# Two tiles padded: where the stationary operands of an attention and MLP kernel lie in SBUF

## The chip, the cores and the metric

The kernel runs on one core of one Trainium2 chip. The metric is device time in microseconds, the median of several runs of one program. One execution was also recorded by the profiler; that execution has a time of its own.

## The reference

Attention with a band mask, then an MLP whose activation is piecewise: zero below -1, a square between, the identity above 1.

```python
def _attn_ref(q, k, v):                      # 8 batches, 8 heads, 576 positions, 64 wide
    scores = scale * np.matmul(q, k.transpose(0, 1, 3, 2))
    ...
    mask_plain = (rel >= 0) & (rel < window)                                  # 32
    mask_dil = (rel >= 0) & (rel < window * dilation) & (rel % dilation == 0) # every 4th
    masks = np.stack([mask_plain if h < H // 2 else mask_dil for h in range(H)], axis=0)
    ...
    return np.matmul(attn, v).astype(np.float32)

def _moe_ref(x, w_in, w_out):                # x 4608 x 512, w_in 512 x 2048, w_out 2048 x 512
    h = x @ w_in
    g = np.where(pos, h, np.where(neg, 0.0, (h + beta) ** 2 / (4.0 * beta)))
    return (g @ w_out).astype(np.float32)
```

## The kernel before

The MLP's 4608 tokens are cut into 9 blocks of 512, its 2048 hidden units into 16 slices of 128. A step is one block t and one slice f, 144 steps in all; layer 2 of a step is issued two steps after its layer 1. Each matrix is split into a high part, rounded to float32r, and a low part, the remainder, and three products stand for one: high by high, and each high by the other's low.

`layer1(t, f)` makes 12 matmuls (four pieces of the 512 input columns, three products each) into one PSUM bank. Its stationary operand is 128 columns of `wi[f]`, its moving operand 512 columns of `xh` or `xl`. The bank is then read by VectorE and ScalarE, which form the activation with the help of the tile `y` and leave it as `gh` (high) and `gl` (low). `layer2(t, f)` makes another 12 matmuls: for each of the four groups m of 128 tokens three products, added over all f into the bank of m. Here the stationary operand is 128 columns of `gh` or `gl`, the moving one the 512 columns of `wo[f]`.

The attention of the first 16 heads runs before and beside the first MLP steps, that of the other 48 beside the later ones. TensorE's and the transfers' order is written out by hand: a table of slots puts scores (L207, L230), transposes (L330) and value matmuls (L365) between the layers of certain steps. VectorE, ScalarE and GpSimd are ordered by a scheduler.

A matmul reads both operands from SBUF: the weights are loaded by an instruction of their own (LDWEIGHTS, in the profile the row PEld), which can run while the matmul before is under way.

Where a tile lies is set by the pools: one region for each tag, in the order in which tags are first asked for, each as long as the first tile of that tag (or its largest); `bufs` regions where a tag has several. The first tag after the constants starts at byte 3136 of a partition, which is 64 modulo 256. What follows, with lengths in bytes, so that the remainder modulo 256 can be followed:

- `pt0`, `pt1` 2304 each (9 x 256), three `xh` and three `xl` of 8192 (32 x 256), `qr` 2304: remainder stays 64
- `kr` 608 x 4 = 2432 (9 x 256 + 128): behind it the remainder is 192
- all `wi` and `wo` but the last 4096 (16 x 256), `vt` 3072, between them two score tiles `c` of 3200 (12 x 256 + 128 each, 256 together), `qs` 2304, `kk` 4864, `m` 2048: remainder stays 192 (64 for the second `c` alone)
- `y`, two `gh`, two `gl` of 2048 each, then the last weight block, `wo15`: 192

Steps within a tile (a piece of 128 columns, a high or low half) are multiples of 512 bytes, so they don't change a remainder in the MLP.

Of the kernel before, what the change touches and what calls it, by code (L numbers as in the profile page):

```python
# [19 lines left out]
F32 = mybir.dt.float32  # L23
# [10 lines left out]
KPAD = S + 32  # L34
CLS = S // DIL
TOK = 512
# [8 lines left out]
def body(ctx, tc, q, k, q2, k2, v, mask, eye, w_in, w_out, out):  # L45
# [4 lines left out]
    pool = ctx.enter_context(tc.tile_pool(name="pool", bufs=1))  # L50
# [15 lines left out]
    def borrow(name):  # L66
        return pool.tile([128, 2 * DM], F32, tag=spare.pop(0), name=name)

    def load_pair(n):

        if 0 < n < H:
            qr, kr = borrow(f"qr{n}")[:, :S], borrow(f"kr{n}")[:, :KPAD]
        else:
            tags = ("qs", "kk") if n % 4 else ("qr", "kr")
            qr = pool.tile([128, S], F32, tag=tags[0], name=f"qr{n}")
            kr = pool.tile([128, KPAD], F32, tag=tags[1], name=f"kr{n}")
        nc.sync.dma_start(out=qr, in_=q[n // 2])
        nc.sync.dma_start(out=kr, in_=k[n // 2])
        for j in range(2):
            r = slice(64 * j, 64 * j + 64)  # L80
            heads[n + j] = dict(qs=qr[r], ks=kr[r])

    def load(n):
        qr = pool.tile([128, S], F32, tag="qr", name=f"qr{n}")
        kr = pool.tile([128, KPAD], F32, tag="kr", name=f"kr{n}")
        nc.sync.dma_start(out=qr, in_=q2[n - native])
        nc.sync.dma_start(out=kr, in_=k2[n - native])
        heads[n] = dict(qr=qr, kr=kr)
# [249 lines left out]
    def xtile(t):  # L338
        if t not in xt:
            xt[t] = (  # L340
                pool.tile([128, NC, TOK], F32R, tag="xh", name=f"xh{t}", bufs=3),
                pool.tile([128, NC, TOK], F32R, tag="xl", name=f"xl{t}", bufs=3),
            )
        return xt[t]
# [51 lines left out]
    def layer1(t, f, cs=range(NC), bank=("h", 2)):  # L396
        xh, xl = xtile(t)
        if cs[0] == 0 and (t, f) not in hps:
            hps[t, f] = ps.tile([128, TOK], F32, tag=bank[0], name=f"h{t}_{f}", bufs=bank[1])
        hp = hps[t, f]  # L400
        terms = [(w, x, c) for c in cs for w, x in ((0, xh), (1, xh), (0, xl))]
        for i, (w, x, c) in enumerate(terms):
            PE.matmul(  # L403
                out=hp,
                lhsT=wi[f][:, w, 128 * c : 128 * c + 128],
                rhs=x[:, c],
                start=c == 0 and i == 0,
                stop=c == NC - 1 and i == len(terms) - 1,
            )
        if cs[-1] < NC - 1:  # L410
            return
        del hps[t, f]
        y = pool.tile([128, TOK], F32, tag="y", name=f"y{t}_{f}")
        gh = pool.tile([128, TOK], F32R, tag="gh", name=f"gh{t}_{f}", bufs=2)
        gl = pool.tile([128, TOK], F32R, tag="gl", name=f"gl{t}_{f}", bufs=2)
        with tc.high_priority(offset=60):
            nc.vector.tensor_scalar(  # L417
                out=y, in0=hp, scalar1=-1.0, scalar2=1.0, op0=ALU.max, op1=ALU.min
            )
            nc.scalar.activation(out=y, in_=y, func=AF.Square, bias=half_t, scale=0.5)  # L420

            activated = nc.vector.tensor_tensor(out=hp, in0=hp, in1=y, op=ALU.max)  # L422
            copied = nc.scalar.copy(out=gh, in_=hp)  # L423
            if t == 0:
                last["g", f] = copied, activated
            nc.vector.tensor_tensor(out=gl, in0=hp, in1=gh.bitcast(F32), op=ALU.subtract)  # L426
        gs[t, f] = gh, gl
# [33 lines left out]
    def after_pair(n):  # L461
        softmax(n)
        softmax(n + 1)
        if n + 4 < native:
            load_pair(n + 4)
        elif n + 4 == native:
            load(native)
        else:
            split(native)
            load(native + 1)  # L470

    def after(m):
        if m < nhead - 1:
            split(m + 1)
        if m < nhead - 2:
            load(m + 2)
        softmax(m)
# [23 lines left out]
    nc.vector.memset(half_t, 0.5)  # L501
    borrow_pts()
    load_pair(0)
    nc.sync.dma_start(out=msk, in_=mask.rearrange("k p j -> p k j"))
    load_pair(2)
    nc.sync.dma_start(out=ident, in_=eye)
    load_pair(4)
# [49 lines left out]
    with tc.manual_schedule(engines={mybir.EngineType.PE, mybir.EngineType.SP}):  # L557
# [25 lines left out]
        early_values(4)  # L583
        second = marks()
        layer1(0, 0, range(2))
        early_values(6)
        third = marks()
        behind(second, ("wi", 2))
        layer1(0, 1, range(2))
        scores_pair(H, 0, 4)  # L590
        scores_pair(H, 4, NQ)
# [9 lines left out]
        for s in range(len(steps) + lag):  # L601
            if s == 3:
                for f, src, name in ((12, w_out, "wo"), (13, w_out, "wo"), (14, w_in, "wi")):
                    fetch(f, src, name)
                for f, src, name in ((14, w_out, "wo"), (15, w_in, "wi"), (15, w_out, "wo")):
                    fetch(f, src, name)
            if 0 < s < NF:
                todo = [("wo", s)]
                if s + 3 < NF:
                    todo.append(("wi", s + 3))  # L610
                behind(last["g", max(s - 2, 0)], *todo)
            if s == 2:
                acc[0] = ps.tile([128, DM], F32, tag="acc0", name="acc0_0")
                spin(14, acc[0])
            if s < 2:
                layer1(*steps[s], range(2, NC))
            elif s < len(steps):
                layer1(*steps[s])
            run(2 * s)
            while l2 <= s - lag and l2 < len(steps):  # L620
                layer2(*steps[l2])
                l2 += 1
            run(2 * s + 1)
# [64 lines left out]
```

## Time and profile before

| what | value |
|---|---|
| median of 3 runs | 938.39 us (937.88 to 938.51) |
| profiled execution, its time | 935.99 us |
| profiled execution, its span | 934.2 us |
| mean granted TensorE clock | 0.997 |
| moved from and to HBM | 73.87 MB in packets, 78 GB/s over the span |

The span runs from the first to the last instruction. A busy time is the time in which an engine had at least one instruction under way; matmuls overlap each other, so their mean duration (some 390 ns for 512 columns) is longer than the distance from one start to the next. That distance is what counts for the time, and it is read from the chain of work or from the starts in the timeline. In the chain, a row gives when a piece began, how long it was, its engine and line, and how many instructions it holds.

The costliest other groups, each with its count, busy time, mean of one, and the idle time before it:

```profile
L255 ACT ACTIVATE c<-c 96x128 f32<-96x128 f32 x330 | 129.0, 392 | 118.3 <-DVE c L181 118.3
L422 DVE TENSOR_TENSOR h<-h,y 128x512 f32<-128x512 f32 x144 | 100.6, 699 | 49.7 <-ACT y L420 48.3
L417 DVE TENSOR_SCALAR y<-h 128x512 f32<-128x512 f32 x144 | 99.3, 689 | 62.7 <-PE h L403 61.3
L426 DVE TENSOR_TENSOR gl<-h,gh 128x512 fp32r<-128x512 f32 x144 | 98.5, 684 | 36.9 <-ACT gh L423 36.9
```

These are the readers of the layer-1 bank and the exponentials of attention; the matmul groups are shown further below.

### The profile page before, as it was taken

How to read it: one execution, taken by the hardware profiler on the slowest of the kernel's cores; microseconds unless marked ns; L12 is line 12 of the kernel's file. 1: busy time of each engine (PE TensorE's matmuls, PEld its weight loads, DVE VectorE, ACT ScalarE, POOL GpSimd, SP SyncE). 2: the span in 40 equal slices, each digit the busy share in tenths (PEclk: the TensorE clock that was granted, in tenths of full speed). 3: DMA queues.
4: the chain of work that ended last, by engine and by line, in shares of the span. 5: the costliest groups of instructions: out<-in, count | busy, mean ns of one | idle time of the engine just before them, and what ended most of it. 6: DMA issues, size and time to landing. Idle time of an engine off the chain costs nothing.

```text
span 934.2 us, 14426 instructions
## 1 busy us (share of the span) xinstructions
PE 914.5 (98%) x4886; PEld 742.9 (80%) x4886; DVE 685.2 (73%) x1982; ACT 487.1 (52%) x1336; POOL 239.8 (26%) x155
## 2 busy tenths in 40 slices
PE   7889989999999999999999999999999999999998
PEld 6777778888888888888888888888888888888886
DVE  6898887888888888788887888888887643334333
ACT  6778856555555555555555565555556322222222
POOL 4566543222222222222222222222222000000000
PEclk9999999999999999999999999999999999999999
DMA  9981002212232223112322223222321010001001
GB/s 345 406 304 45 1 27 83 92 59 64 70 115 70 69 70 95 59 57 70 115 70 70 70 61 101 67 69 70 114 70 44 1 45 1 1 1 46 0 1 46
DMA packets 31018, 73.87 MB, mean 79 GB/s; under 512 B 3520, under 2 KB 3808, under 8 KB 30944
## 3 DMA queue, kind: packets, MB, share of 16 engines
q1 hardware_dynamic: 30944, 72.94, 24.0%
q8 instruction: 39, 0.64, 0.3%
q14 instruction: 35, 0.29, 0.1%
HBM read 63.49 MB, written 9.44 MB: 78 GB/s over the span
## 4 chain that ended last, share of the span: by engine, by line
PE 89%; DVE 6%; ACT 3%; issue 1%; POOL 1%; DMA 0%; DVEq 0%; POOLq 0%; ACTq 0%
PE acc L439 41%; PE h L403 40%; PE s L230 4%; PE o L365 3%; DVE c L181 1%; ACT c L255 1%; DVE wo_raw L123 1%; DVE wo_m L126 1%; DVE wi_m L126 1%; DVE c L298 1%; PE t L330 0%; POOL c L291 0%; PE s L164 0%; DVE xl L350 0%; DVE y L417 0%
## 5 line engine op out<-in xcount | busy, mean ns | idle before, releaser
L439 PE MATMUL acc<-wo,gh 128*128 128x512 f32 x1152 | 384.3, 395 | 0.0
L403 PE MATMUL h<-xh,wi 128*128 128x512 f32 x1152 | 361.0, 394 | 0.8 <-DVE gl L426 0.8
L439 PEld LDWEIGHTS acc<-wo,gh 128*128 128x128 f32 x1152 | 216.2, 188 | 48.3
L403 PEld LDWEIGHTS h<-xh,wi 128*128 128x128 f32 x1152 | 209.4, 188 | 42.6 <-DVE gl L426 1.0
L403 PE MATMUL h<-xl,wi 128*128 128x512 f32 x576 | 227.1, 394 | 0.0
L439 PE MATMUL acc<-wo,gl 128*128 128x512 f32 x576 | 224.9, 391 | 0.0
L143 POOL TENSOR_TENSOR kk<-kr,kk 128x608 fp32r<-128x608 f32 x48 | 94.8, 1974 | 417.7 <-ACT kk L139 417.7
L255 ACT ACTIVATE c<-c 96x128 f32<-96x128 f32 x330 | 129.0, 392 | 118.3 <-DVE c L181 118.3
L420 ACT ACTIVATE y<-y,consts 128x512 f32<-128x512 f32 x144 | 104.1, 723 | 124.7 <-DVE y L417 124.7
L423 ACT CAST gh<-h 128x512 fp32r<-128x512 f32 x144 | 84.4, 586 | 128.2 <-PE acc L439 126.1
L417 DVE TENSOR_SCALAR y<-h 128x512 f32<-128x512 f32 x144 | 99.3, 689 | 62.7 <-PE h L403 61.3
L422 DVE TENSOR_TENSOR h<-h,y 128x512 f32<-128x512 f32 x144 | 100.6, 699 | 49.7 <-ACT y L420 48.3
L403 PEld LDWEIGHTS h<-xl,wi 128*128 128x128 f32 x576 | 108.1, 188 | 25.2
L426 DVE TENSOR_TENSOR gl<-h,gh 128x512 fp32r<-128x512 f32 x144 | 98.5, 684 | 36.9 <-ACT gh L423 36.9
L439 PEld LDWEIGHTS acc<-wo,gl 128*128 128x128 f32 x576 | 108.2, 188 | 21.1
L306 DVE STREAM_TRANSPOSE pt<-c 32x192 f32<-32x192 f32 x288 | 106.0, 368 | 5.7
L249 DVE TENSOR_TENSOR c<-s,msk 96x256 f32<-96x256 f32 (+1 forms) x168 | 61.5, 377 | 39.7 <-PE s L230 38.7
L291 POOL TENSOR_TENSOR c<-c 96x768 f32<-96x768 f32 x56 | 83.1, 1484 | 16.7 <-DVE c L290 16.5
L181 DVE CUSTOM_DVE_ANT_0 c<-s,c 96x128 f32<-96x128 f32 x288 | 70.5, 280 | 1.0
L255 ACT ACTIVATION_READ_ACCUMULATOR c<-c 96x1 f32 x330 | 62.0, 188 | 0.0
L349 ACT CAST xh<-o 128x288 fp32r<-128x288 f32 (+8 forms) x112 | 38.5, 382 | 41.0 <-PE o L365 25.8
L230 PEld LDWEIGHTS s<-kk,qs 128*96 128x96 f32 x288 | 46.4, 161 | 15.7
(57 smaller groups left out, 646.1 us busy)
## 6 DMA issues: line engine op xcount, KB each, us to landing
kr<-k_in SPq DMA_DIRECT2D x56, 304.0 KB, 3.2
qr<-q_in SPq DMA_DIRECT2D x56, 288.0 KB, 2.8
vt<-v_in SPq DMA_DIRECT2D x32, 384.0 KB, 3.9
out<-out SPq DMA_DIRECT2D x36, 256.0 KB, 3.1
wi_raw<-w_in SPq DMA_DIRECT2D x16, 512.0 KB, 9.5
wo_raw<-w_in SPq DMA_DIRECT2D x16, 512.0 KB, 9.9
msk<-mask_in SPq DMA_DIRECT2D x1, 144.0 KB, 3.7
ident<-eye_in SPq DMA_DIRECT2D x1, 36.0 KB, 4.7
```

The lines of the kernel that those rows point to most:

```text
L143: nc.gpsimd.tensor_tensor(out=kk[:, 1], in0=hd["kr"], in1=kk[:, 0].bitcast(F32), op=ALU.subtract)
L230: PE.matmul(out=sv[:, t - t0], lhsT=hd["qs"][:, t * QT : (t + 1) * QT], rhs=hd["ks"][:, :, t * QT : t * QT + 128], start=True, stop=True,)
L255: last["act"] = nc.scalar.activation(out=c[:, t], in_=c[:, t], func=AF.Exp, bias=st[:, 0, t : t + 1], scale=-1.0, accum_out=st[:, 1, t : t ...
L291: nc.gpsimd.tensor_tensor(out=c, in0=c, in1=spread(st[:, 2]), op=ALU.mult)
L306: nc.vector.transpose(out=pt[r : r + 32, :, 32 * g : 32 * g + 32], in_=c[32 * g : 32 * g + 32, :, r : r + 32],)
L403: PE.matmul(out=hp, lhsT=wi[f][:, w, 128 * c : 128 * c + 128], rhs=x[:, c], start=c == 0 and i == 0, stop=c == NC - 1 and i == len(terms) - 1,
L417: nc.vector.tensor_scalar(out=y, in0=hp, scalar1=-1.0, scalar2=1.0, op0=ALU.max, op1=ALU.min)
L420: nc.scalar.activation(out=y, in_=y, func=AF.Square, bias=half_t, scale=0.5)
L422: activated = nc.vector.tensor_tensor(out=hp, in0=hp, in1=y, op=ALU.max)
L423: copied = nc.scalar.copy(out=gh, in_=hp)
L426: nc.vector.tensor_tensor(out=gl, in0=hp, in1=gh.bitcast(F32), op=ALU.subtract)
L439: PE.matmul(out=acc[m], lhsT=g[:, r], rhs=wo[f][:, w], start=f == 0 and i == 0, stop=f == NF - 1 and i == len(terms) - 1,)
```

## The change

Two tiles get a longer row, of which the kernel uses the same part as before: the K tile `kr` 48 elements (192 bytes), the MLP's `y` 16 elements (64 bytes). A blank line at the top of the file moves every line number by one.

```diff
@@ load_pair
-            kr = pool.tile([128, KPAD], F32, tag=tags[1], name=f"kr{n}")
+            kr = pool.tile([128, KPAD + 48], F32, tag=tags[1], name=f"kr{n}")[:, :KPAD]
@@ load
-        kr = pool.tile([128, KPAD], F32, tag="kr", name=f"kr{n}")
+        kr = pool.tile([128, KPAD + 48], F32, tag="kr", name=f"kr{n}")[:, :KPAD]
@@ layer1
-        y = pool.tile([128, TOK], F32, tag="y", name=f"y{t}_{f}")
+        y = pool.tile([128, TOK + 16], F32, tag="y", name=f"y{t}_{f}")[:, :TOK]
```

`kr` is now 2624 bytes (10 x 256 + 64), so that what follows it starts at 128 modulo 256; `y` is 2112 (8 x 256 + 64), so that what follows it, `gh`, `gl` and `wo15`, starts at 192 again. Counted from the start of the moving operand to the start of the stationary one, modulo 256:

| matmul | moving at, stationary at, distance before | after |
|---|---|---|
| layer 1: `xh`, `xl` by `wi` | 64, 192, 128 | 64, 128, 64 |
| layer 2: `wo` by `gh`, `gl` | 192, 192, 0 | 128, 192, 64 |
| layer 2, f = 15: `wo15` by `gh`, `gl` | 192, 192, 0 | 192, 192, 0 |
| scores: `kk` or `kr` by `qs` or `qr` | equal, 0 | equal, 0 |
| values: `pt` by `vt` | 64 or 192, 192, 128 or 0 | 64 or 192, 128, 64 or 192 |
| transposes: identity by `c` | 128, 64 or 192, 192 or 64 | 128, 0 or 128, 128 or 0 |

The instructions of every engine and queue, their order and their waits are the same in both programs, so no listing of them is shown.

## The prediction

> **What bounds the kernel now.** I read the engine shares first, to see which engine sets the time, then the slices, to see where it doesn't.
>
> ```profile
> span 934.2 us, 14426 instructions
> PE 914.5 (98%) x4886; PEld 742.9 (80%) x4886; DVE 685.2 (73%) x1982; ACT 487.1 (52%) x1336; POOL 239.8 (26%) x155
> ...
> PEclk9999999999999999999999999999999999999999
> DMA  9981002212232223112322223222321010001001
> ```
>
> TensorE is busy for 98% of the span at its full granted clock; the transfers fill the DMA engines only in the first three slices. Next comes the busy time by stage, in microseconds from the start: stretch, then busy time (and instructions) of PE, its weight loads, DVE, ACT and POOL, clock, DMA share, GB/s.
>
> ```profile
> 0.00:60.00 60.00, 50.53 (x440) 42.13 (x441) 48.57 (x219) 44.98 (x127) 32.96 (x28) 0.97 0.99 378
> 60.00:130.00 70.00, 64.24 (x383) 50.38 (x382) 62.69 (x132) 53.43 (x117) 42.16 (x31) 1.00 0.15 52
> 130.00:700.00 570.00, 570.00 (x3027) 463.55 (x3026) 468.40 (x1429) 320.14 (x955) 156.31 (x93) 1.00 0.26 76
> 700.00:934.00 234.00, 229.70 (x1042) 186.81 (x1040) 105.53 (x205) 68.54 (x137) 8.39 (x5) 1.00 0.05 18
> ```
>
> From 130 us on TensorE never waits until the last 4 us. So the time is a sum of matmul start-to-start distances, and nothing else is late. The chain of work that ended last says of which:
>
> ```profile
> PE 89%; DVE 6%; ACT 3%; issue 1%; POOL 1%; DMA 0%; DVEq 0%; POOLq 0%; ACTq 0%
> PE acc L439 41%; PE h L403 40%; PE s L230 4%; PE o L365 3%; DVE c L181 1%; ACT c L255 1%; DVE wo_raw L123 1%; DVE wo_m L126 1%; DVE wi_m L126 1%; DVE c L298 1%; PE t L330 0%; POOL c L291 0%; PE s L164 0%; DVE xl L350 0%; DVE y L417 0%
> ```
>
> The two MLP layers are 81% of it. Their pace is read from the same chain in order of time (start, length, line, count), late, where only the MLP runs:
>
> ```profile
> 852.42 2.79 PE h L403 x12
> 855.21 2.73 PE acc L439 x12
> ```
>
> and with attention beside it:
>
> ```profile
> 445.07 1.14 PE o L365 x24
> 446.21 2.95 PE acc L439 x12
> 449.16 0.24 PE s L230 x2
> 449.40 2.78 PE h L403 x12
> 452.18 0.24 PE s L230 x2
> 452.42 2.75 PE acc L439 x12
> 455.17 0.24 PE s L230 x2
> 455.41 2.77 PE h L403 x12
> 458.18 2.77 PE acc L439 x12
> ```
>
> A matmul of layer 1 takes 2.79/12 = 0.2325 us and one of layer 2 2.73/12 = 0.2275 us late in the kernel, although both are 128x128 by 128x512 of one type. A step of the MLP (12 and 12) is 5.52 us late; beside attention it is 2.78 + 2.75 = 5.53 (the 2.95 after value matmuls holds about 0.2 us of the switch). I take **5.53 us times 144 steps = 796 us**; the change can only work on these.
>
> **Is there anything above the columns?** Two sizes of moving operand separate a cost per column from one per matmul. The scores of 256 columns take 0.24/2 = 0.12 us each, layer 2's 512 columns 0.2275. The difference, 0.1075 us for 256 columns, is 0.42 ns a column, so 512 columns alone are 0.215 us. **0.0125 us per matmul is over in layer 2, 0.0175 in layer 1**: 12 x (0.0125 + 0.0175) = 0.36 us of each step, 52 us of the kernel. That is the most a change of addresses could remove, if all of it came from addresses, which this estimate (0.12 has two digits) can't show.
>
> The Trainium skill (TensorE: Matmul & The Clock Gate, "Back-to-back issue gap") gives N/2.4 + 2.5 ns for an isolated matmul, 215.8 ns at 512 columns, as an estimate. The trace's late 227.5 and 232.5 lie above it; by that page a step without the excess would be 5.18 us.
>
> **What the weight load does meanwhile** is in the timeline of PE and its loads (start, length, line, tiles):
>
> ```profile
> 860.57 0.39 PE L439 MATMUL acc<-wo,gh 128*128 128x512 f32 x1
> 860.58 0.19 PEld L439 LDWEIGHTS acc<-wo,gl 128*128 128x128 f32 x1
> 860.77 0.69 DVE L417 TENSOR_SCALAR y<-h 128x512 f32<-128x512 f32 x1 [1.48 <-PE h L403]
> 860.81 0.40 PE L439 MATMUL acc<-wo,gl 128*128 128x512 f32 x1
> ```
>
> And the groups of weight loads by shape (count, busy, mean ns of one, idle before):
>
> ```profile
> L439 PEld LDWEIGHTS acc<-wo,gh 128*128 128x128 f32 x1152 | 216.2, 188 | 48.3
> ...
> L230 PEld LDWEIGHTS s<-kk,qs 128*96 128x96 f32 x288 | 46.4, 161 | 15.7
> ```
>
> The load of the next weights starts with the current matmul and ends 0.04 us before the next (860.77 against 860.81). It isn't the limit itself, but both operands are read at once. 128 columns load in 188 ns, 96 in 161: 27 ns for 32, or 0.84 ns a column. The moving operand (0.42 ns) is read at twice that pace.
>
> **The change, part by part.** No instruction is added, removed or moved, on any engine or queue; each access pattern keeps its shape. Only places in SBUF change. Adding up the tile sizes, modulo 256 bytes: before, x (both halves) lies at 64 and wi, wo, gh, gl at 192. So the stationary wi is 128 past the moving x in layer 1, and the stationary gh or gl is 0 past the moving wo in layer 2. After, wi and wo lie at 128, x stays at 64, gh and gl come back to 192: 64 in both layers. One block escapes: wo15 is allocated behind gl, stays at 192, and leaves layer 2 at 0 in 9 of 144 steps.
>
> - Layer 1 and layer 2 (1728 matmuls each, less 108): no row of this kernel has an MLP matmul at 64, so its price is bounded from both sides. The two known ones are 2.79 us a group at 128 and 2.73 at 0: 0.06 for 128 bytes, 0.03 for 64. If price follows the offset round the circle of 256, 64 either lies between the two (2.76), or on the falling side beyond 0 (2.70), or on the rising side beyond 128 (2.82). The lower bound is the columns alone, 12 x 0.215 = 2.58; the upper one is 2.82, or a little over.
> - I take **2.70 in both layers**. The point nearest to the same distance is layer 2's at 0, which is already the lower of the two, and a stationary operand that lies ahead of a stream of twice its pace is met a little later and not at once, while its load is only beginning. It is a choice, not a derivation.
> - Sum: a step falls from 5.53 to 5.40, 0.13 us; times 144 it is **-19 us**. wo15 takes back 9 x 0.03 = 0.3 us.
> - Other matmuls: scores keep 0 (q and k tiles move together). The value matmuls go from 128 and 0 by turns to 64 and 192 by turns; the 24 of them in 1.14 us are 3% of the chain, and 2% of that, the gap between the two layers, is 0.6 us either way. Transposes show as 0%. I put all of it at nothing.
> - Other engines: tiles move by 64 bytes or not at all, and lengths stay. I put this at nothing, hidden under TensorE: DVE has 468 of 570 us in the densest stage. Were TensorE 2% faster there, DVE would be at 84%; at the lower bound (5.16 a step, at most 7% off) at 88%. Without that cover a microsecond on DVE would cost one, but it isn't near.
> - Transfers: the K tiles' rows are longer in SBUF, the bytes moved are the same, and the queue is mostly idle after the third slice.
>
> The profiled execution took 935.99 us (span 934.2 and 1.8 around it), 2.4 under the median of the runs, 938.39. 935.99 - 19 = 917 for a profile like it; 919 against the median. I say **918**.
>
> **Rivals.**
>
> 1. *Nearly the whole excess goes* (2.58 to 2.66 a group). Meetings of the two streams cause all of it, and 64 avoids them. For it: it would explain why the layers differ. Against: the scores, another shape with fewer weight columns, have the same 0.0125 by construction, as a fixed cost would. Price: 0.37 x 144 = -53, 885 us, in full; half of it, 911.
> 2. *Layer 1 only comes to layer 2's level*, 2.73 and 2.73: the 0.0125 is fixed, and any offset but 128 is as good. 5.46 a step, -0.07 x 144 = -10, 928 us.
> 3. *No difference*: either 64 costs the mean (2.76 twice, 5.52 a step: -1, 937 us), or the addresses don't matter and the layers differ by something else, such as the accumulation: layer 1 adds 12 into one bank, layer 2 changes bank after 3. Against the second: the four starts around 860.81 are 0.23 apart with no step. For it speaks a rule. The Trainium skill (SBUF — State Buffer, "Who interferes with whom") says that TensorE has two independent read ports, one per operand, and never waits on anyone. By that rule the change does nothing; the trace's 2.79 against 2.73 doesn't prove it wrong, since banks differ too.
> 4. *Slower*: at twice the pace the moving stream gains 256 bytes on the stationary one twice while 512 bytes of weights load, whatever the offset; the offset only decides where they meet. If a meeting soon after the start, with the stream just filling, costs more than one at the start, 64 is dearer than 128: 2.82 twice, 5.64 a step, +0.11 x 144 = +16, 954 us; at layer 1's present 2.79 twice, 5.58, +7, 945 us. It decides as soon as the mean group is over 2.765.
>
> **How the numbers follow.** Forecast (2.66 to 2.72, 906 to 925): 0.35. Rival 1 (under 2.66): 0.16. Rival 2: 0.14. Rival 3: 0.13. Rival 4: 0.22, of which 0.13 at about 945 and 0.09 at 950 and over. Faster by over 0.2%: 0.35 + 0.16 + 0.14 = 0.65. Within 0.2%, about what a measurement of this kernel can tell from no change: 0.13. Slower: 0.22. The range of 0.8 leaves out the last 0.09 of rival 4 and a little of rival 1's end: 889 to 948.
>
> **What would show it.** In the chain by time, late pieces of L403 and L439 (a line number may shift by one): 2.70 for both is right; 2.73 is rival 2; 2.6 and less rival 1; 2.79 and more rival 4. Unchanged 2.79 and 2.73 say that addresses don't matter. Each sixteenth layer-2 group reads wo15 and should stay at 2.73: a check inside the one trace. Scores should stay at 0.24 for two, value matmuls at 1.14 for 24, loads at 188 and 161 ns, DVE's busy time at 685 us, and PE without a wait from 130 us on. The forecast is wrong if the groups keep their level and the time moves, or if DVE or ACT take longer on the moved tiles.

## The result, and the profile after

The changed kernel takes **943.96 us** (median of 4 runs, 941.68 to 944.95) where the one before, run beside it, takes 938.13 (937.40 to 938.51). The ratio is 1.006 with a 95% interval of 1.004 to 1.0079: **slower by 0.6%, 5.8 us**. The forecast was 918 us, 20 less than before. The profiled execution took 944.31 us (span 942.5).

Engine shares and the chain by line, as shown of before (every line number is now one higher):

```profile
span 942.5 us, 14426 instructions
PE 923.3 (98%) x4886; PEld 743.9 (79%) x4886; DVE 685.6 (73%) x1982; ACT 487.0 (52%) x1336; POOL 241.0 (26%) x155
...
PE acc L440 42%; PE h L404 40%; PE s L231 4%; PE o L366 3%; ACT c L256 1%; DVE c L182 1%; DVE wo_m L127 1%; DVE wo_raw L124 1%; DVE wi_m L127 1%; DVE c L299 1%; PE s L165 1%; PE t L331 0%; DVE xl L351 0%; ACT wi_raw L122 0%; PE s L208 0%
```

TensorE's busy time grew by 8.8 us, about what the span grew (8.3; the profiled execution of before was 2.4 us under its median); VectorE (685.2 to 685.6), ScalarE and GpSimd did the same work in the same time. In the stretch from 130 to 700 us TensorE still never waits, but it gets through fewer instructions, 2989 against 3027:

```profile
130.00:700.00 570.00, 570.00 (x2989) 460.02 (x2989) 464.06 (x1416) 318.73 (x951) 156.00 (x92) 1.00 0.25 74
```

So the matmuls themselves became slower. Which ones, the chain in order of time says (start, length, line, count), late in the kernel:

```profile
851.41 2.77 PE acc L440 x12
854.18 2.80 PE h L404 x12
856.98 2.80 PE acc L440 x12
```

and beside attention:

```profile
449.39 1.14 PE o L366 x24
450.53 2.99 PE acc L440 x12
453.52 0.23 PE s L231 x2
453.75 2.79 PE h L404 x12
456.55 0.24 PE s L231 x2
456.78 2.78 PE acc L440 x12
```

Layer 1 stays where it was (2.79 and 2.80 for 2.79 late). Layer 2 rises from 2.73 to 2.80 late, from 2.75 to 2.78 beside attention. The one group of 2.77 is the step with wo15, which stayed at distance 0: the check inside the trace answers, though only by part of the way. By its single starts it steps by 224 to 236 ns at first and by 226 or 227 only at its last three matmuls. A late step takes 5.59 us for 5.52; beside attention 2.79 + 2.78 = 5.57 for 5.53. Added up over the starts of all matmuls in the two profiled executions, layer 2 takes 7.2 us more, layer 1 1.4 more and the scores 0.3 less, together the 8.3 by which the spans differ.

### The profile page after: what moved, and what is told of

Same layout as the page of the kernel before. It is cut to its first block, busy times and chain, and to the rows that moved or that the text cites. A ratio compares the mean times of both kernels' runs of the same rounds, so it can differ in the third digit from the quotient of the medians.

```text
span 942.5 us, 14426 instructions
## 1 busy us (share of the span) xinstructions
PE 923.3 (98%) x4886; PEld 743.9 (79%) x4886; DVE 685.6 (73%) x1982; ACT 487.0 (52%) x1336; POOL 241.0 (26%) x155
## 4 chain that ended last, share of the span: by engine, by line
PE 91%; DVE 5%; ACT 3%; issue 1%; POOL 0%; DMA 0%; DVEq 0%; POOLq 0%; ACTq 0%
PE acc L440 42%; PE h L404 40%; PE s L231 4%; PE o L366 3%; ACT c L256 1%; DVE c L182 1%; DVE wo_m L127 1%; DVE wo_raw L124 1%; DVE wi_m L127 1%; DVE c L299 1%; PE s L165 1%; PE t L331 0%; DVE xl L351 0%; ACT wi_raw L122 0%; PE s L208 0%
## 5 line engine op out<-in xcount | busy, mean ns | idle before, releaser
L440 PE MATMUL acc<-wo,gh 128*128 128x512 f32 x1152 | 388.3, 398 | 0.0
L440 PE MATMUL acc<-wo,gl 128*128 128x512 f32 x576 | 227.7, 395 | 0.0
```

Of the source, the lines that this page charges most:

```text
L440: PE.matmul(out=acc[m], lhsT=g[:, r], rhs=wo[f][:, w], start=f == 0 and i == 0, stop=f == NF - 1 and i == len(terms) - 1,)
```

## The experiments

**The curve by itself.** Attention and MLP are left out: one tile of float32r holds everything, and groups of 24 equal matmuls run back to back, each group with its own distance. Two lines of code take turns, so that every group is a piece of its own in the chain.

```python
def a(at, far, n, cols, width):
    st = 1024 + at + far          # elements of 4 bytes
    for i in range(n):
        PE.matmul(out=acc[:cols, :width], lhsT=w[:, st : st + cols], rhs=w[:, at : at + width], start=True, stop=True)
```

> Attention and MLP are left out: only groups of 24 matmuls, 128x512, one after the other, from one tile, with the stationary operand at a chosen distance behind the moving one (0 to 512 bytes), then with the moving operand at 64 and 128 bytes, then with 64 and 32 stationary columns. Theory 1 (the distance modulo 256 sets the pace): a group takes 24 x 0.2267 = 5.44 us at 0, 256 and 512, and 24 x 0.2333 = 5.60 at 64 and 128, wherever the moving operand starts; 192 is open. Theory 2 (the place of the moving operand sets it): all distances alike for one moving start, other starts differ. Theory 3 (most of the excess over 0.215 us is a fixed cost of a matmul): groups with 64 and 32 columns take 5.4 as well; if loads collide with the stream, 32 columns come near 24 x 0.216 = 5.18.

Some groups of the chain of that run, in order: distances 0, 64, 128, 192 and 256; then with the moving operand at 64, distances 0 and 64; then 32 stationary columns at 0 and 64:

```profile
26.90 5.44 PE acc L38 x24
...
48.97 5.59 PE acc L38 x24
...
71.34 5.60 PE acc L38 x24
...
93.65 5.50 PE acc L38 x24
...
115.80 5.44 PE acc L38 x24
...
143.38 5.48 PE acc L33 x24
148.86 5.60 PE acc L38 x24
...
209.76 5.56 PE acc L33 x24
215.32 5.56 PE acc L38 x24
```

All sixteen distances, length of the group of 24 in us:

| bytes | 0 | 16 | 32 | 48 | 64 | 80 | 96 | 112 |
|---|---|---|---|---|---|---|---|---|
| us | 5.44 | 5.45 | 5.59 | 5.60 | 5.59 | 5.57 | 5.61 | 5.60 |
| **bytes** | **128** | **144** | **160** | **176** | **192** | **208** | **224** | **240** |
| us | 5.60 | 5.60 | 5.59 | 5.52 | 5.50 | 5.59 | 5.60 | 5.46 |

Distance theory holds: 256 and 512 bytes are 0 again (5.44, 5.45), and a moving operand at 64 or 128 bytes gives the same distances the same lengths within 0.04 us. At 0 only the first few matmuls are slower; at 128 these groups settle at 231.7 ns a matmul where the first one settled at 233.3. Theory 2 falls for these starts. The granted clock is 1.00 in all these groups. The curve is a plateau of 5.6 with a valley at 0 and 16 on either side, and a shallow one about 192. It is no smooth valley: a group at 8 bytes takes 5.54. Nothing is under 5.44. The second half of theory 3 falls too: with 32 stationary columns, a quarter of the load, the stream takes 5.56 at 0 as at 64, nowhere near 5.18. Most of the excess isn't what loads do to the stream; the full load at distance 0 even has a shorter step than hardly any load.

**What makes the excess.** In the same frame, one operand or the other repeats a single column (a "still" operand), or both; then bf16; then 16 stationary columns and fewer moving ones.

> Attention and MLP are left out; groups of 24 matmuls as in the first such run. First the control at distance 0 (5.44 us at 0.2267 each), then the same with a stationary operand whose 128 columns are one repeated column, then with a moving operand that repeats one column, then both; then bf16 at distances 0, 64, 128, 192 bytes; then 16 and 32 stationary columns with 512 down to 320 moving ones. Theory A (two address streams meet in SBUF): a still operand takes the meetings away, so that at least the dependence on distance goes, and the excess over 0.215 us shrinks; bf16, with half the bytes, shows little of either. Theory B (the excess is a fixed cost of a matmul at full clock, with the distance only shifting it): still operands and bf16 keep 0.227 or more. By the width rows, a fixed excess gives the same nanoseconds at every width; meetings of streams give less for narrower ones.

In the chain, in this order: control; still stationary; still moving at 0 and at 128 bytes; bf16 at 64; 16 stationary columns with 512 and with 320 moving ones:

```profile
26.05 5.44 PE acc L50 x24
31.49 5.55 PE acc L40 x24
...
48.13 5.25 PE acc L50 x24
...
58.62 5.25 PE acc L50 x24
...
79.56 5.18 PE acc L50 x24
...
95.10 5.56 PE acc L40 x24
...
119.52 3.49 PE acc L50 x24
```

A still moving operand runs at 5.25 (218.7 ns a matmul) whatever the distance; a still stationary one, whatever its distance, at 5.55. bf16 takes 5.18 to 5.19 at all four distances. So most of the excess belongs to the moving stream of 4-byte words that runs over addresses; some 3 ns a matmul over bf16 stay with a still one. And it grows with the width: with 16 stationary columns, from 512 to 320 moving ones, the group loses 2.07 us, which is 2.07/24/192 = 0.449 ns a column, against 5.18/24/512 = 0.422 for bf16. There it is a slower pace, not a fixed cost per matmul. Theory A was right about the distance, bf16 and the width, and wrong in that a still stationary operand doesn't shorten the step (5.55 for 5.44). Theory B is out: still moving operands and bf16 are under 0.227.

**Over what stretch of addresses.** The moving operand repeats a window of its first columns.

> Attention and MLP are left out; groups of 24 matmuls of 128x512. The moving operand now repeats a window of 512, 256, 128, 64, 32, 16, 8 or 4 columns until 512 have passed: with 16 stationary columns (hardly any load), then with 128 at distance 0, then with 128 at distance 64. Then moving and stationary together 4, 8, 16 and 32 bytes further on. Theory A (the moving stream of 4-byte words is itself slower than 0.42 ns a column when it runs over addresses, and the load only shifts it): with 16 columns 5.56 us a group as before from a window of 64 words (256 bytes) up, and a fall to about 5.25 for windows that stay within one line of memory; with 128 columns the difference between the two distances goes where the window is short. Theory B (loads cost it): the 16-column groups are at 5.25 for all windows, which the last run already speaks against.

With 16 stationary columns, windows of 64, 32, 16 and 8 words:

```profile
47.60 5.55 PE acc L43 x24
53.15 5.68 PE acc L38 x24
58.82 5.84 PE acc L43 x24
64.67 5.23 PE acc L38 x24
```

With 128 stationary columns at distance 0 the windows of 256, 128 and 64 words all take 5.44, at distance 64 all 5.60; at 32 words both 5.68, at 8 and 4 words both 5.24 to 5.25. A window of 256 bytes is as good as the whole row, which fits a period of 256 bytes. Up to 32 bytes the stream is fast and blind to the distance. A window of 64 bytes is slowest of all, which no theory had said.

The last groups keep distance 0 and start both operands 4, 8, 16 and 32 bytes further on in the tile, with 128 stationary columns:

```profile
185.48 5.71 PE acc L38 x24
191.18 5.56 PE acc L43 x24
196.74 5.54 PE acc L38 x24
202.28 5.47 PE acc L43 x24
```

By single starts they settle at 237.8, 231.2, 231.1 and 226.7 ns a matmul. So the distance isn't all: at distance 0 a start 4, 8 or 16 bytes on is slower too, one of 32, 64 or 128 isn't (but for the first few matmuls). The tiles of the kernels here start at multiples of 64.

**One layer at a time.** First the K tile's pad without that of `y`, then the pad of `y` without that of the K tile (distances of layer 1 and layer 2: 64 and 0; 128 and 64).

```diff
-            kr = pool.tile([128, KPAD], F32, tag=tags[1], name=f"kr{n}")
+            kr = pool.tile([128, KPAD + 48], F32, tag=tags[1], name=f"kr{n}")[:, :KPAD]
...
-        kr = pool.tile([128, KPAD], F32, tag="kr", name=f"kr{n}")
+        kr = pool.tile([128, KPAD + 48], F32, tag="kr", name=f"kr{n}")[:, :KPAD]
```

> The K tile's pad alone: layer 1 at distance 64, layer 2 at 0, with wo now at 128. Theory 1: late groups 2.79 (layer 1) and 2.73 (layer 2), time as before, 936 to 940. Theory 2 (wo at 128 is slow): layer 2 at 2.80, 944, the whole loss. Theory 4 (the longer K rows slow something else): over 940 with unchanged groups.

```diff
-        y = pool.tile([128, TOK], F32, tag="y", name=f"y{t}_{f}")
+        y = pool.tile([128, TOK + 16], F32, tag="y", name=f"y{t}_{f}")[:, :TOK]
```

> The pad of y alone: layer 1 stays at distance 128, layer 2 goes to 64, wo stays at 192. Theory 1: layer 2 at 2.80 late, layer 1 at 2.79: the whole loss, 943 to 945. Theory 2 (wo at 192 is fast): 938.

Layer 1 alone: 941.82 us, ratio 1.0041 (1.0026 to 1.0056). Layer 2 alone: 943.42, 1.0058 (1.0041 to 1.0075). The second is as theory 1 says, 2.79 to 2.80 late. The first isn't: late groups are 2.80 and 2.74, within 0.01 of what was expected, yet the time rises by 3.5 us. The chain beside attention, layer 1 alone, shows where:

```profile
452.89 2.80 PE h L403 x12
455.69 0.23 PE s L230 x2
455.92 2.79 PE acc L439 x12
```

Layer 2, still at distance 0, takes 2.79 after two score matmuls where it took 2.75, and layer 1 2.80 for 2.78. Over all starts of the two profiled executions that is 3.6 us more in layer 2, whose distance didn't change, and 2.2 in layer 1. By the letter the time over 940 with unchanged late groups is theory 4's sign, but it is the matmuls themselves that step slower beside attention (TensorE waits nowhere from 130 to 700 us), and the kernel below, whose K rows are longer too, is faster. Nor do the two parts add up: 0.41% and 0.58% would be 1.0%, both together are 0.6%. My reading, which the two kernels with changed scores further below test: the distance sets the pace a layer comes to, and what ran before it sets how long that takes.

**Distance 0 in both layers**, by a pad of 128 bytes on the K tile alone.

```diff
-            kr = pool.tile([128, KPAD], F32, tag=tags[1], name=f"kr{n}")
+            kr = pool.tile([128, KPAD + 32], F32, tag=tags[1], name=f"kr{n}")[:, :KPAD]
...
-        kr = pool.tile([128, KPAD], F32, tag="kr", name=f"kr{n}")
+        kr = pool.tile([128, KPAD + 32], F32, tag="kr", name=f"kr{n}")[:, :KPAD]
```

> K tile padded by 128 bytes alone: stationary and moving start alike modulo 256 in both layers (all at 64). Theory 1: late groups of 2.72 to 2.73 in both layers, 0.06 less per step, and no slow entry into layer 2: about 10 us faster than before, 928. Theory 2 (moving at 64 is slow, as in layer 1 before): 2.79 in both, 944.

> The kernel with distance 0 in both layers once more, with more rounds, as the one to compare the next with: 929 to 931, ratio 0.990 to 0.993.

929.96 us, ratio 0.9908 (0.9889 to 0.9927), and again 930.26, 0.9921 (0.9907 to 0.9935). Both layers in the chain, late:

```profile
855.32 2.72 PE acc L439 x12
858.04 2.72 PE h L403 x12
```

and beside attention:

```profile
451.54 2.73 PE acc L439 x12
454.27 0.24 PE s L230 x2
454.51 2.73 PE h L403 x12
```

2.72/12 is 226.7 ns, the 5.44/24 of the bare groups. Theory 2, by which x at 64 is slow, falls again.

**Distance 192 in both layers** (K tile + 16 elements, `y` + 48, in the same lines).

> Distance 192 in both layers (K tile padded by 64 bytes, y by 192). If the group rows of the first such run (228.9 ns a matmul at 192) hold inside the kernel: late groups of 2.75, a step of 5.50 against 5.53, so 932 to 936. If only 0 is good and the kernel's two streams behave differently: 2.79, 944.

936.40 us, ratio 0.9979 (0.9970 to 0.9988), late groups of 2.75 to 2.77 and 2.75 where the bare groups had promised 2.75. The curve carries over; the time is 0.4 us past the slow end of what was expected. Six layer-1 groups beside attention, behind scores, take 2.80: a group doesn't always come to the bare pace.

**Everything moved by 64 bytes**, distances kept.

```diff
-    consts = const.tile([128, 16], F32, name="consts")
+    consts = const.tile([128, 32], F32, name="consts")
```

> Constants padded by 64 bytes: every tile of the pools moves by 64, all distances stay as before (128 in layer 1, 0 in layer 2). Distance theory: late groups 2.79 and 2.73 and the time of before, within 0.2%. Place theory: x moves to 128 and wo to 0, and the groups change.

937.67 us, ratio 0.9995 (0.9985 to 1.0004); late groups 2.79 and 2.73. No difference, as the distance theory says.

**The scores before a layer.** The kernel with distance 0 in both layers leaves the score matmuls, which read 128 columns of each half of `kk`, at distance 0 for the first half and 128 for the second (the table of the change has the first half alone). Two kernels change the second: to 0, and to 64 (the latter with a gap behind the tile that keeps all that follows in place). In the latter the moving half starts 192 bytes past the stationary operand; counted from the moving to the stationary one, as everywhere else here, that is 64, though the expectation below calls it 192.

```diff
-        kk = pool.tile([128, 2, KPAD], F32R, tag="kk", name=f"kk{n}")
+        kk = pool.tile([128, 2, KPAD + 32], F32R, tag="kk", name=f"kk{n}")[:, :, :KPAD]
```

> As the run with distance 0 in both layers, and the low half of the K tile padded by 128 bytes so that the scores' second 128 columns lie at distance 0 too. If the score matmuls answer to the distance as the MLP's do: two scores take a little under 0.24 us, some 1 to 2 us in all, 928 to 929. If not: 930 as in the other run.

```diff
-        kk = pool.tile([128, 2, KPAD], F32R, tag="kk", name=f"kk{n}")
+        kk = pool.tile([128, 2 * KPAD + 64], F32R, tag="kk", name=f"kk{n}")[:, : 2 * KPAD + 32]
+        kk = kk.rearrange("p (a j) -> p a j", a=2)[:, :, :KPAD]
```

> Distance 0 in both MLP layers, and the scores' second 128 columns at distance 192 (with 128 in the kernel it is made from, and 0 in the one that lost 5 us). Theory: the scores hand the next layer a state, and the layer needs 2 to 10 matmuls to come to its lasting pace. Then late groups stay at 2.72 in any case, and beside attention they lie between 2.72 and 2.77: 927 to 936, by how long the entry lasts. If the 5 us were lost for another reason (the longer K tile), this kernel, whose K tile is longer too, gives 935.

The first was a miss: 934.97 us, ratio 0.9965 (0.9953 to 0.9978), 5 us more than without it. The second gives **927.51 us, 0.9895 (0.9877 to 0.9914)**, the fastest of all. The chain beside attention of the kernel with 0:

```profile
454.39 0.24 PE s L230 x2
454.63 2.77 PE acc L439 x12
457.40 0.24 PE s L230 x2
457.64 2.77 PE h L403 x12
460.40 2.72 PE acc L439 x12
```

and of that with 64:

```profile
450.28 2.72 PE acc L440 x12
453.00 0.24 PE s L231 x2
453.24 2.72 PE h L404 x12
455.96 2.72 PE acc L440 x12
```

The two scores take 0.24 us each way, and TensorE waits nowhere from 130 to 700 us in either kernel. What differs is the layer behind them: 2.77 or 2.72, with the MLP's own distances the same. In the first kernel only the layer that follows another layer (460.40) has 2.72. By the starts of single matmuls in the trace, in the first kernel a layer after scores steps by 224 to 236 ns and reaches 227 only at its last two or three; with the second half at 128 it reaches 227 after two; at 64 it begins there. The longer tile isn't to blame: it is longer in both. Why 64 hands over best of the three isn't shown; for the MLP's own matmuls it is a slow distance.

## Why the prediction was wrong

- **The bound was right.** TensorE waits nowhere from 130 us on until the last 4, the change worked almost wholly on the two MLP layers, scores stayed at 0.23 to 0.24 for two, value matmuls at 1.14 for 24, loads at 188 and 161 ns, the other engines at their times. The pace of the load holds as well: in the bare groups 128 columns load in 188 ns and 32 in 108, 0.83 ns a column.
- **The step that failed: "I take 2.70 in both layers".** It laid a straight line through two points, 2.79 at 128 and 2.73 at 0, and continued it beyond 0. Measured by the bare groups, 64 gives half of 5.59, 2.80. The curve has no slope to continue: it is a plateau from 32 to 160 with 0 in a valley a few tens of bytes wide. The reason given with the choice, that a stationary operand ahead of the stream is met later, was never a price, and the one distance it was applied to came out dearer than 0.
- **"Is there anything above the columns?" was wrong too.** It read 0.0125 us a matmul as over, removable at most. That came from 0.12 us, a number of two digits, for the scores. Widths in one frame, with 16 stationary columns, give 0.449 ns a column instead of 0.42: most of the excess is the moving stream's own pace, which no distance removed. The best kernel found gains 10.5 us (938.02 to 927.51 beside each other), not up to 52. Rival 1 had no ground.
- **Rival 4 happened**, given 0.22. Its milder price, 2.79 twice and 945 us, was nearly exact (943.96), with some luck: it took over layer 1's price at 128, and 64 lies on the same plateau. Its mechanism, that the place where the two streams meet decides, is borne out only in so far as place decides; that meetings with the load cost the time isn't, since with 16 or 32 stationary columns the stream is as slow.
- **My reading of the rule in rival 3** fails in this case: the Trainium skill (SBUF — State Buffer, "Who interferes with whom") gives TensorE two independent read ports and lets it wait on no one, which I read as no effect of addresses; the same matmuls took 5.44 or 5.60 us by distance alone. Whether the ports are where it arises isn't shown.
- **A step the prediction lacked**: that a layer's pace depends on what ran just before it. It parted kernels of equal MLP distances by 0.7% (ratios 0.9965 and 0.9895). That the scores "keep 0" was true of their first half alone; the second stayed at 128, so it changed nothing here.
- **The range** is wider in chance than it says: by its own chances it leaves out 0.09 and a little, and so holds about 0.9, not 0.8.
- **Left open**: which part of the memory or of TensorE holds the 256 bytes, why 192 is a shallow valley, why starts 4 to 16 bytes on are slow, why a window of 64 bytes is slowest, and what it is that one run of matmuls hands the next. The runs show the pattern and not its cause.

## What to carry to other kernels

Where a TensorE-bound kernel streams float32r operands as this one does, put the stationary operand at the same address as the moving one modulo 256 bytes (here 0.8 to 0.9% of the whole kernel for a pad of 128 bytes), with both at multiples of 64, as here, and measure the curve with bare groups before choosing any other distance. Two points of an unknown periodic curve tell nothing of a third. Matmuls of another shape between such groups hand them a state, so a change to those is judged by the layer that follows as well.

## What the runs showed of the hardware

- By single starts in the trace, a 128x512 float32r matmul steps by 226.7 ns at a distance of 0, 16 or 240 bytes and by 230 to 234 at most others; with a still moving operand by 218.7; in bf16 by 5.18/24 = 215.8. The last is what the Trainium skill gives for an isolated matmul (TensorE: Matmul & The Clock Gate, "Back-to-back issue gap": N/2.4 + 2.5, 215.8), and the trace agrees, though here it is the step of a stream; the same section puts a stream of 512 columns at about 131 ns a matmul, which no run here comes near. float32r has a pace of its own.
- The settled pace isn't always one: at distance 128 (384 is the same modulo 256) four bare groups of the same shape settled on two. One took 233.3 ns, behind a group at 112 bytes; three took 231.7, behind groups at 64, with the moving operand at 0, 64 and 128 bytes. So it isn't the moving operand's place; what ran before fits.
- With a full weight load at distance 0 the step is shorter (5.44 a group) than with a load of 16 columns (5.56), although the load reads eight times as much; with a still stationary operand it is 5.55. At 0 the load's addresses shorten the step, at 64 (5.59) they lengthen it.
